# Fewer unread products ahead of the first read one, the others placed anew

## The chip, the cores and the metric

The kernel runs on one core of one Trainium2 chip. The metric is the device time of one execution in microseconds, the median of several runs. A core has several engines that run side by side, each with its own queue in a fixed order: PE multiplies matrices (its weight loads are shown as PEld), DVE, ACT and POOL work element by element, and SP issues most of the transfers (DMA). An instruction whose operands are not there makes its engine wait, and all behind it in that queue wait with it.

## The reference

The reference has two halves. The first is a gated linear recurrence with complex gates over 768 steps, for 4 batches of 8 heads with 48 channels; the second is a mixer over the tokens and a two-layer network over the 384 channels.

```python
scale = np.minimum(mag, 0.999) / (mag + 1e-06)        # mag = |a_re + i a_im|
a_re_n, a_im_n = (a_re * scale, a_im * scale)
for t in range(S):
    new_re = ar * S_re - ai * S_im                     # ar, ai: the gates of step t
    new_im = ar * S_im + ai * S_re
    S_re, S_im = (new_re + kv, new_im)                 # kv: outer product of k and v
    y[:, :, t] = np.einsum('bhd,bhde->bhe', q[:, :, t], S_re)
...
h = xt @ U @ V                                         # x: y with the heads side by side
u = x + h.transpose(0, 2, 1)
ch = np.maximum(u @ w_ch1, 0.0) @ w_ch2
return (u + ch).astype(np.float32)
```

## The kernel before

The sequence is cut into chunks of 128 steps, six to a batch, 24 in all, and two neighbouring chunks make a group. For each group `gates` turns the inputs `a_re` and `a_im` into logarithms of magnitudes and angles. `magnitudes_of` has ACT and DVE work in turn until the logarithms stand in `GL`. `within` then has PE sum them along the chunk, with the fixed matrices `mid` and `fore` as weights (L674, tiles `es ps` and `ef ps`), and ACT takes exponentials of the sums into `es` and `ef`. `of_blocks` does the same for sums over blocks (L712, `tot`, weights `total`). `angles` sums the angles along the chunk (L776 and L779, `ph`), and ACT and DVE reduce them (`F`, L782) for the sines and cosines `cs`. In the first group the two chunks go through these steps one by one.

`prep` scales queries and keys with `es` and `cs` (DVE, L377, `QKC`), PE transposes them (L834, `tr`) and ACT copies the transposes out (L845, `QK`). `chain` does the attention of the chunk: products within blocks (L881 and L884, `inner`; L948, `corners`), the state (L973, `dk`), and the chunk's output (L1004 and L1012, `y`), which ACT copies to `xo`. When the six chunks of a batch are done, `mixer` works on pairs of them: the low-rank mixing (`rank`, `mixed`, `uTp`), and the two layers (L1094 `up` or L1152 `few`; L1241 and L1284 `down`).

The weights of the two layers are loaded in pieces into a staging ring of two tiles (`stage`), and `single` has DVE and ACT put each piece into its place by five word operations (L556 to L562 in the early pieces).

What each engine does in which order is not left to a scheduler. Every operation is added to a `Plan` with its engine and kind, and the table `ORDER` gives each a place, a number; `order` sorts all operations by that place. The lists of all engines follow from the sorted list, and instructions of one engine keep that order.

The table `SPARE` belongs to the same places. An entry `37: 79` says that 79 units of unread product stand ahead of the operation at place 37. A unit multiplies 128 columns of the identity matrix by the identity; `idle` makes products of up to four units (512 columns) out of a run of units, at L1414. They read `ident` alone, write one tile in PSUM that no instruction reads, and stand in PE's queue like every other product. In float32 each product shows as two passes in the trace, each with its own weight load. Place 37 is the first read product of the program, the `es ps` sum of the first chunk.

```python
        out += [-1] * SPARE.get(at[n], 0) + [n]
...
    def idle(k):
        ...
        nc.tensor.matmul(out=spare[0][:, :k], lhsT=ident, rhs=ident.unsqueeze(1).to_broadcast([128, k, 128]), start=True, stop=True)
...
        while run:
            idle(min(run, 4))
            run -= min(run, 4)
        plan.ops[n][4]()
```

Places that the prediction names: 37, 43, 45, 46 and 56 (first group's sums: `es ps`, `ef ps` and `tot`), 84 and 93 (its angles), 113 to 122 and 144 (transposes of the first two chunks), 127 and 147 (`inner` of the first chunk), 245 and 255 (the two halves of `dk` of the second chunk), 246 (L779 of the fourth chunk), 272 and 275 (the transposes of the third chunk), 276 (`y` of the second).

## Time and profile before

| | |
|---|---|
| Runs (us) | 646.06, 649.92, 652.8 (median 649.92) |
| The profiled execution (us) | 645.24 |
| Its span (us) | 643.5 |
| PE busy | 633.6 us, 98% |
| DVE busy | 510.2 us, 79% |
| ACT busy | 398.5 us, 62% |
| Unread products (L1414) | 81 products, 162 passes, 1.4 to 126.3 us |
| First read product (L674) | 21.40 us |
| First product of the two layers (L1094) | 128.69 us |

The span runs from the first to the last instruction of the profiled execution; its time as a run is 1.7 us more. A busy share counts an engine's instructions whether or not somebody needs them, so PE's 98% holds the unread products too. The profile shows no column for the rate of one pass: the granted clock stands at 1.00 throughout, and a slower stretch of PE is read from the distance between neighbouring passes. In the timeline neighbouring instructions of one kind are merged, and a merged line shows the shape of the first alone.

### The profile page before, as it was taken

The page shows a single profiled execution, that of the slowest core. Times are in us where ns is not written, and L with a number is a line of the kernel's source. Part 1 is how long each engine was busy: PE and PEld are TensorE (multiplying, and loading weights), DVE is VectorE, ACT ScalarE, POOL GpSimd, SP SyncE. Part 2 cuts the span into 40 slices and gives each one's busy share as a digit, 9 for nine tenths or more (in the row PEclk, how much of TensorE's full clock was granted, in tenths as well). Part 3 has the DMA queues.
Part 4 walks back from the last instruction along what each step waited for, and adds up shares of the span by engine and source line. Part 5 has one row for each costly group of instructions (what it writes and reads, how often), then busy time and mean ns, then how long its engine had stood idle before and what let it go on. Part 6 is the DMA issues. An engine that isn't in the chain of part 4 may idle for free.

```text
span 643.5 us, 23479 instructions
## 1 busy us (share of the span) xinstructions
PE 633.6 (98%) x10384; PEld 535.4 (83%) x10384; DVE 510.2 (79%) x923; ACT 398.5 (62%) x765; POOL 39.1 (6%) x79
## 2 busy tenths in 40 slices
PE   9999999999999999999999999999999999999998
PEld 3566667686789988888989988888999998999997
DVE  4599999968999989768876968788999894573653
ACT  4599999888887897766868585868532422202010
POOL 5000000000001000020010000010100000000200
DMA  8367556456125341431540430521212010000101
GB/s 206 67 163 162 117 110 148 118 151 138 35 43 119 74 82 39 85 79 30 105 88 5 92 85 13 105 67 21 50 45 46 12 32 8 1 13 1 38 7 43
DMA packets 173685, 45.74 MB, mean 71 GB/s; under 512 B 167632, under 2 KB 170384, under 8 KB 173584
## 3 DMA queue, kind: packets, MB, share of 16 engines
q1 hardware_dynamic: 171376, 39.90, 29.5%
q0 software_dynamic: 2208, 4.35, 2.0%
q8 instruction: 81, 1.33, 0.9%
q14 instruction: 20, 0.16, 0.1%
HBM read 33.59 MB, written 4.72 MB: 60 GB/s over the span
## 4 chain that ended last, share of the span: by engine, by line
PE 87%; DVE 8%; issue 2%; ACT 1%; DMA 1%; SPq 0%; POOL 0%; DVEq 0%; POOLq 0%
PE down L1284 24%; PE up L1094 18%; PE few L1152 11%; PE spare L1414 5%; PE tr L834 3%; PE y L1012 3%; PE dk L973 3%; PE inner L884 3%; PE down L1241 2%; PE inner L881 2%; PE y L1004 2%; PE tot L718 2%; DVE QKC L377 2%; PE mixed L1066 1%; DVE QK L377 1%
## 5 line engine op out<-in xcount | busy, mean ns | idle before, releaser
L1094 PE MATMUL up<-uT,w 128*128 128x256 f32 x504 | 115.9, 383 | 0.0
L377 DVE TENSOR_TENSOR QK<-QK,T 112x512 f32<-112x512 f32 (+1 forms) x144 | 102.3, 730 | 7.1 <-PE inner L881 3.3
L1094 PEld LDWEIGHTS up<-uT,w 128*128 128x128 f32 x504 | 93.8, 190 | 13.0 <-ACT h L374 0.3
L1284 PE MATMUL down<-w,h 128*128 128x192 f32 x396 | 73.3, 331 | 0.0
L374 ACT ACTIVATE gate<-gate 128x768 f32<-128x768 f32 (+1 forms) x89 | 69.8, 798 | 4.9 <-DMA gate<-in_a_im_dram 1.9
L845 ACT COPY QK<-tr 112x512 f32<-112x512 f32 x96 | 52.5, 586 | 32.2 <-PE tr L834 31.2
L1284 PEld LDWEIGHTS down<-w,h 128*128 128x128 f32 x396 | 64.4, 190 | 2.5 <-issue 1.7
L1414 PE MATMUL spare<-ident 128*128 128x512 f32 (+3 forms) x162 | 62.2, 506 | 1.8 <-POOL ident masks.py:199 1.4
L1414 PEld LDWEIGHTS spare<-ident 128*128 128x128 f32 x162 | 29.4, 196 | 27.9 <-issue 21.9
L377 DVE TENSOR_TENSOR QKC<-qk,cs 128x768 f32<-128x768 f32 x48 | 45.6, 953 | 7.9 <-PE tr L834 4.4
L380 DVE TENSOR_TENSOR xo<-down,xo 128x192 f32<-128x192 f32 (+1 forms) x79 | 30.1, 386 | 24.2 <-PE down L1284 23.8
L1160 ACT COPY h<-few 128x512 f32<-128x512 f32 x30 | 17.2, 587 | 51.4 <-PE few L1152 51.4
L1284 PE MATMUL down<-stage 128*128 128x192 f32 x198 | 38.0, 332 | 0.0
L1152 PE MATMUL few<-gate,w 128*128 128x128 f32 x280 | 35.9, 276 | 0.0
L834 PEld LDWEIGHTS tr<-ident,QKC 64*112 64x112 f32 x768 | 25.6, 130 | 10.9 <-issue 4.7
L759 POOL DMA_DIRECT2D gate<-F x15 | 12.4, 823 | 355.0 <-DVE F L782 208.5
L953 ACT COPY AT<-corners 32x128 f32<-32x128 f32 x96 | 24.2, 255 | 15.4 <-PE corners L948 13.9
L1152 PEld LDWEIGHTS few<-gate,w 128*128 128x128 f32 x280 | 33.6, 192 | 0.2
L834 PE MATMUL tr<-ident,QKC 64*112 64x64 f32 x768 | 32.4, 222 | 0.9 <-ACT QK L845 0.7
L1228 POOL DMA_DIRECT2D out_dram<-xo x32 | 19.0, 613 | 231.5 <-DVE xo L380 173.4
L374 ACT ACTIVATE es<-es ps 128x384 f32<-128x384 f32 x48 | 21.9, 491 | 17.8 <-PE es ps L674 11.3
L1284 PEld LDWEIGHTS down<-stage 128*128 128x128 f32 x198 | 31.8, 190 | 0.8 <-DVE QKC L377 0.2
(156 smaller groups left out, 1251.9 us busy)
## 6 DMA issues: line engine op xcount, KB each, us to landing
stage<-in_moe_w_ch_dram SPq DMA_DIRECT2D x12, 768.0 KB, 5.4
gate<-in_a_im_dram SPq DMA_DIRECT2D x24, 192.0 KB, 3.7
gate<-in_a_re_dram SPq DMA_DIRECT2D x24, 192.0 KB, 3.3
qk<-in_q_dram SPq DMA_DIRECT2D x24, 192.0 KB, 3.2
qk<-in_k_dram SPq DMA_DIRECT2D x24, 192.0 KB, 3.2
VP<-in_v_dram SPq DMA_DIRECT2D x24, 192.0 KB, 3.4
AT<-DG SPq DMA_DIRECT2D x96, 32.0 KB, 2.1
T<-E SPq DMA_DIRECT2D x48, 48.0 KB, 2.8
```

Of the source, the lines that this page charges most:

```text
L374: return nc.scalar.activation(out=o, in_=i, func=f, **kw)
L377: nc.vector.tensor_tensor(out=o, in0=a, in1=b, op=OP.mult)
L380: nc.vector.tensor_tensor(out=o, in0=a, in1=b, op=OP.add)
L834: nc.tensor.transpose(out=get(*ps[r])[0:DQ, h], in_=get(*qkc)[at, h].rearrange("p u d -> p (u d)")[:, 0:DQ], identity=ident[at, at], tile_ ...
L845: nc.scalar.copy(out=to, in_=a)
L884: nc.tensor.matmul(out=get(*ps0)[j * BLK:(j + 1) * BLK, h, 0:3 * HB], lhsT=k_of(h, j * BLK, BLK), rhs=q_of(h, (PL, 3), (1, HB), at=j * HB) ...
L953: ACT(0.36, RR, lambda r=r, u=u: nc.scalar.copy(out=get(*ATi).rearrange("p (a u) t -> p a u t", u=2)[r:r + BLK, :, u, BLK:2 * BLK], in_=ge ...
L973: nc.tensor.matmul(out=get(*dk[r])[x:end, h], lhsT=get(*ks)[at, h, x // DP, 0:end - x], rhs=get(*VPi)[at, h], start=True, stop=True, tile_ ...
L1094: nc.tensor.matmul(out=get(*ps)[:, e], lhsT=w1[:, f, (ff + e) * 128:(ff + e + 1) * 128], rhs=get(*uT)[:, f], start=(f == 0), stop=(f == KD ...
L1152: nc.tensor.matmul(out=get(*ps)[:, q], lhsT=w()[:, q * 128:(q + 1) * 128], rhs=v[0](), start=(n == 0 and q == 0), stop=True, skip_group_ch ...
L1284: nc.tensor.matmul(out=get(*to)[:, part], lhsT=x(j), rhs=y[:, j], start=(first and j == 0), stop=(j == KH - 1), skip_group_check=not first)
L1414: nc.tensor.matmul(out=spare[0][:, :k], lhsT=ident, rhs=ident.unsqueeze(1).to_broadcast([128, k, 128]), start=True, stop=True)
```

## The change

Only the table `SPARE` is changed. At place 37 stand 20 units where 79 stood: five products of 512 columns in place of 19 of them and one of 384. Behind place 37 there were 150 units and are now 152. Of these 110 keep their places, 40 are taken away and 42 are added. Most entries change by one to six units; the largest changes are at places 272 (0 to 14) and 275 (13 to 3). The order of all other operations on every engine is the same.

```diff
-SPARE = {37: 79, 43: 1, 45: 2, 46: 1, 56: 1, 84: 14, 93: 1, 113: 10, 116: 5, 122: 5, 127: 2, 140: 1, 144: 5, 147: 4, 173: 1, 175: 1, 205: 13, 235: 1,
-         246: 1, 255: 7, 275: 13, 287: 1, 302: 2, 305: 6, 325: 3, 340: 2, 367: 3, 376: 4, 391: 2, 416: 9, 423: 1, 433: 2, 449: 2, 455: 1, 469: 2, 488:
-         11, 492: 2, 501: 1, 510: 2, 531: 1, 571: 2, 573: 2}
+SPARE = {37: 20, 43: 2, 45: 4, 56: 1, 84: 15, 93: 3, 113: 11, 116: 2, 122: 4, 127: 3, 144: 7, 147: 3, 161: 1, 170: 2, 205: 13, 245: 2, 255: 1, 272:
+         14, 275: 3, 276: 1, 302: 1, 305: 6, 325: 3, 334: 1, 340: 1, 367: 3, 376: 4, 402: 3, 416: 5, 423: 5, 433: 2, 449: 3, 469: 3, 488: 9, 492: 3,
+         501: 1, 510: 2, 534: 1, 571: 2, 573: 2}
```

## The prediction

> **What bounds the kernel now.** I read the page's busy times and slices first. PE, the matmul engine, looks like the bound over the whole span, but part of its work here is products that nobody reads, so its share says little. The slices (16.1 us each) show that DVE and ACT are half idle in the first two and then nearly full.

> ```profile
> PE 633.6 (98%) x10384; PEld 535.4 (83%) x10384; DVE 510.2 (79%) x923; ACT 398.5 (62%) x765; POOL 39.1 (6%) x79
> ...
> PE   9999999999999999999999999999999999999998
> ...
> DVE  4599999968999989768876968788999894573653
> ACT  4599999888887897766868585868532422202010
> ```

> Second, the waits between 21.4 and 45 us (engine and line, what it waited for, us in total, times, longest). The two longest are one event: ACT waits 11.3 us for the first read product (es ps, L674), and DVE waits as long for an ACT step queued behind that one.

> ```profile
> ACT es L374 <- PE es ps L674: 11.3, 1, 11.3
> DVE GL L380 <- ACT gate L374: 11.3, 1, 11.3
> ```

> Third, the timeline of the first 31 us (start, duration, both us, engine, line). PE runs 40 unread passes from 1.43 to 21.4 us. The product behind them needs GL, which DVE had finished at 9.18 + 0.56 = 9.74 us. Up to 6.71 us the weight loads (PEld) stand 0.855 us apart, from 7.46 us on 0.43 us: each pass took twice as long in the first 6 us.

> ```profile
> 1.43 20.14 PE L1414 MATMUL spare<-ident 128*128 128x512 f32 x40 [1.43 <-POOL ident masks.py:199]
> ...
> 5.86 0.34 PEld L1414 LDWEIGHTS spare<-ident 128*128 128x128 f32 x1 [0.52 <-issue]
> ...
> 6.71 0.34 PEld L1414 LDWEIGHTS spare<-ident 128*128 128x128 f32 x1 [0.52 <-issue]
> ...
> 7.46 0.19 PEld L1414 LDWEIGHTS spare<-ident 128*128 128x128 f32 x1 [0.41 <-issue]
> ...
> 7.88 0.19 PEld L1414 LDWEIGHTS spare<-ident 128*128 128x128 f32 x1 [0.24 <-issue]
> ...
> 9.18 0.56 DVE L380 TENSOR_TENSOR GL<-GL,gate 128x384 f32<-128x384 f32 x1
> ...
> 10.06 0.92 ACT L374 ACTIVATE gate<-gate 128x384 f32<-128x384 f32 x2
> ...
> 11.36 0.56 DVE L560 TENSOR_SCALAR w<-w 128x768 uint32<-128x768 uint32 x1
> ...
> 20.76 0.19 PEld L1414 LDWEIGHTS spare<-ident 128*128 128x128 f32 x1 [0.24 <-issue]
> ...
> 21.40 0.81 PE L674 MATMUL es ps<-GL,mid 128*128 128x384 f32 x2
> ...
> 22.25 0.49 ACT L374 ACTIVATE es<-es ps 128x384 f32<-128x384 f32 x1 [11.27 <-PE es ps L674]
> ```

> Last, the busy times by stretch (after the two times: the length, then busy us of PE, PEld, DVE, ACT and POOL with counts). From 32 to 130 us DVE works 27.86 + 34.09 + 32.97 = 94.92 of 98 us: there DVE sets the pace, with ACT close behind, and unread products fill what PE would have idle. From about 130 us on the read products fill PE.

> ```profile
> 11.00:21.40 10.40, 10.40 (x26) 4.64 (x25) 0.91 (x3) 0.00 (x0) 1.19 (x4) 1.00 0.38 107
> ...
> 32.00:60.00 28.00, 27.37 (x552) 17.81 (x551) 27.86 (x50) 27.06 (x48) 0.00 (x0) 1.00 0.62 144
> 60.00:95.00 35.00, 34.04 (x823) 22.55 (x822) 34.09 (x55) 33.21 (x66) 0.00 (x0) 1.00 0.58 132
> 95.00:130.00 35.00, 33.29 (x777) 24.05 (x776) 32.97 (x57) 31.94 (x61) 0.00 (x0) 1.00 0.58 140
> ```

> **Part 1: the products ahead of the first read one.** A unit is 128 columns, four units make one product, and each product is two passes. At place 37 there were 79 units (20 products, 40 passes); there are now 20 (5 products, 10 passes). When is PE free? The 40th pass loaded its weights at 20.76, and es started at 21.40, 0.64 us later. The 10th loaded at 7.88, so PE is free at about 8.52. When can es start? GL is there at 9.74; the next es followed its GL (DVE, 23.18 + 0.56 = 23.74) at 23.89, so 0.15 us later: 9.89 us. PE thus pauses 1.4 us, and es starts 11.51 us earlier than at 21.40. "mid", the other operand, was ready at 6.24 us on POOL.

> What follows on ACT: es starts on ACT 22.25 − 21.40 = 0.85 us after es on PE, so at 10.74, but ACT is busy until 10.06 + 0.92 = 10.98. So ACT goes on at 10.98 in place of 22.25: 11.27 us, the whole of its wait. DVE's own wait ends with ACT's next step (22.64 + 0.51 = 23.15, less 11.27 is 11.88), while DVE is busy until 11.36 + 0.56 = 11.92: it goes on at 11.92 in place of 23.18, 11.26 us earlier. Neither has a wait left there. What was hidden behind those 11.27 us: on POOL "total", done at 11.97, first needed by L712, which moves from 25.82 to 14.55; and transfers. The DMA engines fell quiet at 15.2 us, and DVE's first use of the second weight piece (L556) moves from 26.69 to 15.43. That is 0.2 us behind the last byte, so it still fits. SP's queue had stood from 10.68 to 25.78 waiting to refill an input area; that wait ends with DVE's work, so SP and every later load move up with it. **Term: −11.27 us.**

> **Part 2: the units behind it.** There were 150, there are 152. At 0.43 us a pass a unit costs 0.215 us, so 0.43 us more PE time in all, in a stretch where DVE sets the pace. I went through the places with the trace. In the first group the added units at 43, 45 and 93 end when the product behind them gets its operand anyway: es of the second chunk waits for GL until 23.89, L779 for F until 32.65. The added one at 113 makes the transposes up to 0.2 us late (they started at 35.73, just when QKC was there, at 34.72 + 0.96 = 35.68). The large move is at 255, 272 and 275 (7, 0, 13 become 1, 14, 3). In old times: dk (L973) comes about 1.1 us earlier; the 14 units end near 66.75, so the next transposes (L834) start there and not at 65.00; ACT reads them (L845) at 67.89, behind a table load that ends at 67.6, and they are done at 67.4. The transposes after them waited for that ACT copy at 68.6 and 69.0, before as after. So the 3 us of products shift inside time that ACT's queue covers; uncovered, the 1.75 us would be late at DVE's QK steps. The other places change by one to four units (0.2 to 0.9 us), in pairs that cancel within a few products.

> Bounds: at worst every added unit lies on the path and no removed one gives anything back. There are 42 of them, 42 × 0.215 = +9.0 us. At best PE never again holds DVE up and all DVE idleness from 32 to 130 us goes: 98 − 94.92 = 3.1, so −3.1 us. I take **+0.2 us**, the one delay found above, since the rows show DVE full and the moved units beside it.

> **Part 3: the pause.** Whether PE keeps its faster passes over a 1.4 us pause and products with gaps in them, no row of before shows: after 7.46 us PE never waits longer than 0.8 us until its work is done. The bounds are nothing, and one renewed slow spell as long as the first (1.43 to about 7.3, 5.9 us), which costs half its length, 2.9 us. I take nothing: the pause is short beside the 5.9 us it took to speed up. [...]

> **Sum.** −11.27 + 0.2 + 0 = −11.1 us. The profiled execution took 645.24 us (span 643.5 and 1.7 around it), so it would take 634.1. It was faster than all three runs shown (646.06, 649.92, 652.8); their median less the same sum is 649.92 − 11.1 = **638.8 us**.

> **Rivals.**
> A. *PE falls back to slow passes once* at the pause. For: the first passes were slow without a busy stretch behind them, and PE, with 9.83 us busy in 21.4 to 32 us, has small gaps just there. Against: the pause is a quarter of the 5.9 us. Price up to 2.9 us: 641.7.
> B. *Loads become the wait.* In the first 32 us 2.20 + 1.11 + 1.08 = 4.39 MB moved; they now have 20.7 us. At the 200 GB/s of the first 11 us that takes 22.0 us, 1.3 us too long: 640.1. Against: 7 to 11 us ran at 279 GB/s, and part of those bytes are needed only later.
> C. *The moved units land on the path.* All of the +9.0: 647.8. For: the unread products stand in PE's one queue, as at the start, and the 14 at place 272 are a long block. Against: the walk above, and the 40 units taken away elsewhere.
> D. *Slower: PE stays at slow passes* from the pause on until the dense products (L1094, 128.69 us). Working without a break at half rate, half of every microsecond is lost, so it decides from 22 us of slow passes on (22 / 2 = 11). Held to the dense products it adds the PE time from 21.4 to 130 once more, 9.83 + 27.37 + 34.04 + 33.29 = 104.5: 743. Against: PE with a backlog works without a pause, and 5.9 us of that sped it up.
> That PE's order is unchanged is excluded: in the changed kernel five products stand ahead of L674, and the other engines' orders are the same.

> **How the numbers follow.** Forecast 0.85, A 0.05, B 0.05, C 0.03, D 0.02. The range: the lower end is the profiled execution less the sum, 634.1, rounded down to 634; it holds the best bound, 649.92 − 11.27 − 3.1 = 635.6. The upper end is the slowest run shown less the sum, 641.7, with some 1.8 for part of A or C: 643.5. C in full and D are left out. A measurement of this kernel can tell about 1% (6.5 us) from no change. The forecast and A and B lie beyond that (1.7, 1.3 and 1.5%), together 0.95, of which I take off 0.08 because the three runs shown differ by 1%: faster 0.87. C and that 0.08, less a hundredth for slower: 0.10. Slower: D and that hundredth, 0.03.

> **What would show it.** Right: ten passes, then a pause of about 1.4 us; L674 at about 9.9 us; ACT's es at about 11.0 without an 11 us wait; the first L1094 near 128.69 − 11.1 = 117.6 us; everything behind it as long as before; the span near 632.4. A: weight loads again 0.85 us apart behind the pause. B: DVE L556 or ACT's input steps waiting for DMA. C: DVE or ACT waiting for PE near 54 us, where L834 now stands behind 14 units. The forecast is wrong if the first L1094 comes later than 122 us, or if the stretch behind it grows.

## Result and profile after

The median of twelve runs went from 649.45 to 641.54 us; the ratio of the kernels is 0.989, with a 95% interval of 0.9853 to 0.9928 (one disturbed run of the twelve is left out of it). In a second set of runs it was 0.9893 (0.9857 to 0.993). So the change saves about 7 us where 11.1 were forecast. The profiled execution took 638.75 us, 6.5 less than the one before, and 4.7 more than the 634.1 of the sum.

The page's slices (one digit for a fortieth of the span) show the hole of DVE and ACT in the first two slices gone:

```profile
span 637.0 us, 23399 instructions
...
DVE  6999898877999989569886868689999894573653
ACT  6899897898887887767678576777442331202010
```

The timeline of the first 25 us (start, duration, engine, line; in brackets the idle time ahead and what ended it):

```profile
1.42 7.54 PE L1414 MATMUL spare<-ident 128*128 128x512 f32 x10 [1.42 <-POOL ident masks.py:199]
...
8.53 0.94 ACT L374 ACTIVATE gate<-gate 128x384 f32<-128x384 f32 x2 [0.90 <-DMA gate<-in_a_im_dram]
...
10.29 0.56 DVE L380 TENSOR_TENSOR GL<-GL,gate 128x384 f32<-128x384 f32 x1
...
10.99 0.88 PE L674 MATMUL es ps<-GL,mid 128*128 128x384 f32 x2 [2.03 <-DVE GL L380]
...
12.00 0.47 ACT L374 ACTIVATE es<-es ps 128x384 f32<-128x384 f32 x1
...
12.94 0.55 DVE L380 TENSOR_TENSOR GL<-GL,gate 128x384 f32<-128x384 f32 x1
```

Ten passes, a pause, and es at 10.99 us where it was 21.40. ACT and DVE go on at 12.00 and 12.94 without the 11 us wait, 10.25 and 10.24 us earlier than before. Those 10 us still stand at the transposes that moved from 71.70 to 61.42 us. At the first dense product only 5.65 are left. PE's own timeline shows where they went:

```profile
61.42 0.66 PE L834 MATMUL tr<-ident,QKC 64*112 64x64 f32 x16
...
67.43 0.44 PE L834 MATMUL tr<-ident,QKC 64*112 64x64 f32 x8 [0.72 <-issue]
...
77.45 0.34 PE L881 MATMUL inner<-QK 112*16 112x16 f32 x25 [0.68 <-issue]
...
96.05 1.02 PE L973 MATMUL dk<-VP,QKC 64*48 64x48 f32 x54 [1.13 <-issue]
...
105.94 0.87 PE L718 MATMUL tot<-total,GL 128*96 128x32 f32 x8 [1.31 <-issue]
...
123.04 2.32 PE L1094 MATMUL up<-uT,w 128*128 128x256 f32 x10
```

PE stops inside runs of products whose operands are there ("issue": nothing that the profile shows was waited for). Number all that stands in PE's queue in order of time, the passes, the weight loads and 168 semaphore and drain instructions: seven such waits (0.72, 0.18, 0.68, 0.23, 1.13, 0.44 and 1.31, 4.69 us in all) stand ahead of numbers 1985, 2241, 2497, 2753, 3265, 3521 and 3777, each 193 plus a multiple of 256. In the kernel before the same stretch has one, the last of these lines; the first is ACT's step on the second chunk's a_im, there without a wait:

```profile
7.41 0.92 ACT L374 ACTIVATE gate<-gate 128x384 f32<-128x384 f32 x2
...
71.70 0.66 PE L834 MATMUL tr<-ident,QKC 64*112 64x64 f32 x16
...
88.49 1.12 PE L1414 MATMUL spare<-ident 128*128 128x512 f32 x2 [0.41 <-issue]
```

The queue row of the changed kernel's page says what has that size:

```profile
q8 instruction: 81, 1.33, 0.9%
```

1.33 MB in 81 transfers is 16,384 bytes each. PE's queue holds 20,856 entries (2 × 10,344 passes and weight loads and the 168 others); behind the first 193 that is 80.7 times 256. The kernel below with 10,232 passes shows 80 such transfers, the one with 10,420 shows 82. So I read these counts as PE getting its instructions in blocks of 256. In the trace, from 62 to 106 us, a block's transfer starts 1.1 to 4.1 us after PE has entered the block before it, takes 0.9 to 1.5 us, and PE goes on no earlier than 1.26 us after its end. The blocks ahead of the seven waits lasted 3.5 to 6.5 us, the waits at their ends included. I call these pauses block waits and add up those over 0.1 us from number 449 on.

### The profile page after: what moved, and what is told of

It reads as the page before. It is cut to its first block, busy times and chain, and to the rows that moved or that the text cites. A ratio compares the mean times of both kernels' runs of the same rounds, so it can differ in the third digit from the quotient of the medians.

```text
span 637.0 us, 23399 instructions
## 1 busy us (share of the span) xinstructions
PE 621.6 (98%) x10344; PEld 529.0 (83%) x10344; DVE 510.1 (80%) x923; ACT 399.0 (63%) x765; POOL 37.3 (6%) x79
## 3 DMA queue, kind: packets, MB, share of 16 engines
q8 instruction: 81, 1.33, 0.9%
## 4 chain that ended last, share of the span: by engine, by line
PE 88%; ACT 4%; DVE 4%; issue 2%; DMA 1%; SPq 1%; DVEq 0%; ACTq 0%
PE down L1284 24%; PE up L1094 18%; PE few L1152 11%; PE tr L834 4%; PE dk L973 4%; PE y L1012 3%; PE spare L1414 3%; PE inner L884 3%; PE down L1241 3%; PE y L1004 2%; PE inner L881 2%; PE tot L718 2%; PE mixed L1066 1%; PE uTp L1079 1%; PE corners L948 1%
## 5 line engine op out<-in xcount | busy, mean ns | idle before, releaser
L1094 PE MATMUL up<-uT,w 128*128 128x256 f32 x504 | 115.6, 383 | 0.0
L1094 PEld LDWEIGHTS up<-uT,w 128*128 128x128 f32 x504 | 94.2, 190 | 12.4
L845 ACT COPY QK<-tr 112x512 f32<-112x512 f32 x96 | 52.5, 586 | 33.7 <-PE tr L834 32.8
L374 ACT ACTIVATE gate<-gate 128x768 f32<-128x768 f32 (+1 forms) x89 | 69.8, 798 | 5.2 <-DMA gate<-in_a_im_dram 2.5
L1414 PE MATMUL spare<-ident 128*128 128x512 f32 (+3 forms) x122 | 49.4, 517 | 1.4 <-POOL ident masks.py:199 1.4
L380 DVE TENSOR_TENSOR xo<-down,xo 128x192 f32<-128x192 f32 (+1 forms) x79 | 30.2, 386 | 24.2 <-PE down L1284 23.7
L834 PEld LDWEIGHTS tr<-ident,QKC 64*112 64x112 f32 x768 | 25.8, 130 | 14.3 <-issue 5.8
L1414 PEld LDWEIGHTS spare<-ident 128*128 128x128 f32 x122 | 22.0, 199 | 18.7 <-issue 12.8
L834 PE MATMUL tr<-ident,QKC 64*112 64x64 f32 x768 | 32.8, 223 | 2.0 <-issue 0.7
L374 ACT ACTIVATE h<-up 128x512 f32<-128x512 f32 x42 | 24.6, 592 | 11.6 <-PE up L1094 11.6
```

The costliest lines, as they stand in the source:

```text
L374: return nc.scalar.activation(out=o, in_=i, func=f, **kw)
L380: nc.vector.tensor_tensor(out=o, in0=a, in1=b, op=OP.add)
L834: nc.tensor.transpose(out=get(*ps[r])[0:DQ, h], in_=get(*qkc)[at, h].rearrange("p u d -> p (u d)")[:, 0:DQ], identity=ident[at, at], tile_ ...
L845: nc.scalar.copy(out=to, in_=a)
L1094: nc.tensor.matmul(out=get(*ps)[:, e], lhsT=w1[:, f, (ff + e) * 128:(ff + e + 1) * 128], rhs=get(*uT)[:, f], start=(f == 0), stop=(f == KD ...
```

## Experiments

First the two parts by themselves, the units in another cut, and none behind the first product. The rival of the block theory is that the moved units cost the 4.7 us.

**Part 1 alone.**

```diff
-SPARE = {37: 79, 43: 1, 45: 2, 46: 1, ...   # kernel before
+SPARE = {37: 20, 43: 1, 45: 2, 46: 1, ...
```

> Only place 37 is changed (79 units to 20); behind it the units stand as in the kernel before. The changed kernel's first dense product (L1094) came at 123.04 us, 5.65 us earlier than before, though es had come 10.4 us earlier; 4.7 us went between about 62 and 106 us in eight waits of PE, each at a multiple of 256 of its passes and weight loads. Theory of the instruction blocks: PE gets its instructions in blocks of 256 (16,384 bytes a transfer) and waits when one is late, whatever stands in it; here es comes at about 10 to 11 us, and the first L1094 at 128.69 - 10.3 = 118.4 us plus whatever such waits this execution has, 0 to 5 us; the waits it has stand at multiples of 256 again, so at other operations, since the units are others. Time 637 to 644 us. Rival, the moved units: they alone cost the 4.7 us; then here no wait of that kind, first L1094 at 118.4 +- 0.5 us and a time 4.7 us below the changed kernel's.

Measured: median 641.79 us, ratio 0.9947 (0.9912 to 0.9983); es at 10.11 and the first L1094 at 124.96 us. Eight block waits, 6.00 us in all, 5.02 of them ahead of L1094; the longest, 2.0 us, stands inside "corners" (L948) and not at "tot", at the same number 3777. The moved units are not there and the loss is: the rival falls.

**Part 2 alone.**

```diff
-SPARE = {37: 20, 43: 2, 45: 4, 56: 1, ...   # changed kernel
+SPARE = {37: 79, 43: 2, 45: 4, 56: 1, ...
```

> Place 37 keeps its 79 units; behind it the units stand as in the changed kernel. Theory of the instruction blocks: es at 21.4 us as before, the first L1094 at 128.7 us plus its own block waits (0 to 5 us), the time that of the kernel before within 1%. Rival, the moved units: they cost 4.7 us here too, with waits or late products at the same operations as in the changed kernel, first L1094 at 133.4 us, time 4.7 us above before.

Measured: 649.06 us, ratio 1.0048 (1.0017 to 1.0078), first L1094 at 133.07 us, just where the rival put it. But what came late was not a product behind a unit. PE's longest waits from 22 to 135 us:

```profile
PE dk L973 <- issue: 2.6, 1, 2.6
PE inner L881 <- issue: 1.3, 1, 1.3
```

They stand at the numbers 1985 and 3521, with a third at 3265: 4.34 us. Less these, L1094 comes at 128.7 us as in the kernel before, although es had come 1.47 us earlier here (19.93 us). Most of that lead went into slow passes: the granted clock is 0.50 from 76.06 to 79.47 us, right behind the longest wait. The moved units thus cost time by way of the blocks: five products fewer stand ahead of number 1985, and the boundaries fall elsewhere.

**Products of two units.**

```diff
-            idle(min(run, 4))
-            run -= min(run, 4)
+            idle(min(run, 2))
+            run -= min(run, 2)
```

> The changed kernel with the same units at the same places, issued as products of at most two units (256 columns) in place of four: the same columns and PE time, but about 25 products, so 100 passes and weight loads, more by 67 us. Theory of the instruction blocks: every block boundary falls some 20 to 130 instructions earlier in the program; PE's waits that end by no operand stand again exactly 256 passes and weight loads apart, at other operations than L834, L884, L881, L948, L973, L881, L718 in that order, and their sum may be anything from 0 to 8 us; time 636 to 645 us. Rival, the moved units or the operations themselves: the waits stay at the same operations with the same lengths (0.7, 0.2, 0.7, 0.2, 1.1, 0.4, 1.3 us), the time stays that of the changed kernel.

Measured: 637.18 us (four runs), ratio 0.9868 (0.9815 to 0.9921). Block waits at 2753, 3521, 4289 and 8897, in other operations than in the changed kernel, 3.97 us in all: as the block theory has it. The same profile shows the prediction's rival A. The ten first products ended sooner, PE paused 2.68 us ahead of es, and soon after its passes were slow (the granted clock is 0.50 from 11.79 to 15.21 us):

```profile
10.42 0.88 PE L674 MATMUL es ps<-GL,mid 128*128 128x384 f32 x2 [2.68 <-DVE GL L380]
...
11.57 1.26 PE L674 MATMUL ef ps<-GL,fore 128*128 128x384 f32 x2
12.62 1.91 PE L1414 MATMUL spare<-ident 128*128 128x256 f32 x4
14.33 1.24 PE L674 MATMUL es ps<-GL,mid 128*128 128x384 f32 x2
15.41 0.81 PE L674 MATMUL ef ps<-GL,fore 128*128 128x384 f32 x2
```

**No unread product behind place 37.**

```diff
-SPARE = {37: 20, 43: 2, 45: 4, ...
+SPARE = {37: 20}
```

> Twenty units at place 37 as in the changed kernel, and no unread product behind it. PE has 56 products (224 passes and weight loads) less and idles where they stood. If PE keeps its faster passes (weight loads 0.43 us apart for 512 columns and the dense L1094 rows as long as before): DVE sets the pace up to 120 us, the first L1094 comes at 117 to 119 us plus block waits, time 635 to 642 us. If it falls back to slow passes wherever it idles (the rival A and D of the prediction, and the reason for such products): read products of the stretch 10 to 120 us take up to twice as long (L674 0.88 us becomes about 1.6), DVE and ACT wait for PE, and the first L1094 comes later than in the changed kernel, by up to half of PE's 70 us of read products: time 645 to 680 us.

Measured: 647.47 us, ratio 1.0038 (1.0007 to 1.0069), first L1094 at 131.47 us. The busy times by stretch (the last but two column is the granted clock) show PE idling, and its clock falling with it:

```profile
20.00:40.00 20.00, 13.59 (x265) 8.95 (x264) 18.60 (x33) 17.05 (x28) 0.00 (x0) 0.67 0.54 140
...
60.00:80.00 20.00, 15.50 (x376) 11.89 (x376) 18.04 (x32) 17.07 (x30) 0.00 (x0) 0.66 0.41 90
```

The changed kernel shows 1.00 there. So the 152 units behind place 37 are worth more than the whole gain of the change; the 59 that it takes away were the idle ones.

Next, whether the block waits come again, and what makes a block late.

**The changed kernel and the kernel before once more.**

> The changed kernel once more, with the kernel before on the same chip. So far an execution's time less its block waits (waits of PE at the multiples of 256 passes and weight loads, up to the first dense products) was 645.24 - 0.41 = 644.8 us before and 638.75 - 4.69 = 634.1 us after. Theory of the instruction blocks: the sum of the waits differs from one execution to the next, so this profile shows es at 10 to 11 us, the first L1094 at 118.3 us plus its sum, a time of 634 us plus its sum, and a sum between 1 and 8 us; the median against before lies between -4 and -11 us. Rival, the execution profiled was an odd one: its waits do not come again, the first L1094 is at 118 to 119 us.

> The kernel before once more, for its block waits. Theory of the instruction blocks: its runs lie between 643 and 653 us because the sum of its block waits differs; this execution's time less its sum is 644.8 +- 1 us, whatever its time. Rival: the kernel before has no such waits beyond the 0.4 us of its first profile, and its scatter comes from elsewhere; then a time of 649 us would show with a sum below 1 us.

Measured: 638.65 us median. The profiled execution of the changed kernel (640.21 us) has its waits ahead of the same seven numbers, 1.04, 0.46, 0.95, 0.50, 0.31, 0.64 and 1.86, in all 5.76 us. The kernel before (644.5 us) has one of 0.20. Less their waits the two took 634.45 and 644.30 us, as the first profiles did (634.06 and 644.63). So the sum is not an accident of one execution but belongs to the program; the second theory, that the scatter of the kernel before comes from such waits, was not put to the test, because this execution was one of its short ones.

**Lighter weight pieces, and no placing of the diagonal blocks.**

```diff
-                out=get("raw", p)[:, at:end].rearrange(...), in_=a.bitcast(U32)),
+                out=get("raw", p)[:, at:end].rearrange(...)[:, :, 0:n], in_=a.bitcast(U32)[:, :, 0:n]),   # n: an eighth for p > 4
```

> The changed kernel, with each weight piece from the sixth on loaded to one eighth (the other columns keep what an earlier piece left in the staging ring); every instruction of PE, DVE and ACT stays. If a block is late because data transfers stand ahead of it: with some 3 MB less between 45 and 115 us the time from entering a block to the start of the next block's transfer (median about 1.4 us, up to 4.1 in that stretch) falls below 1 us in most blocks, the block waits up to the first L1094 sum to less than 1.5 us, and the first L1094 comes at 118 to 120 us. If a block is late whatever the data do: the sum stays at 3 to 5 us and the first L1094 near 123 us.

```diff
-            SP(0.2, ("place", i), lambda js=js, to=to: nc.sync.dma_start(out=get(*ATi)[js, :, to], ...
+            continue
```

> The changed kernel without the transfers that place the diagonal blocks (AT from DG, L935, four to a chunk); those parts of AT keep zeros. The two longest delays of a block, 4.1 us each, overlapped such transfers (69.4 to 72.5 and 100.4 to 102.4 us). If those small transfers hold the blocks up: no delay over 3 us, the block waits sum to less than 2.5 us, first L1094 at 118 to 120.5 us. If not: delays of 4 us remain, the sum stays at 3 to 5 us. In both cases the y products (L1004) no longer wait for a transfer, which was 1.2 us at 257 us.

Measured: with light pieces the waits at 1985, 2241 and 2497 are gone and the one at 2753 is 0.14; those at 3265, 3521 and 3777 stay at 1.13, 0.99 and 1.86, so the sum is 4.12 up to L1094, which comes at 122.96 us. Sum and time are those of the second expectation, but four of the seven waits went all the same: the delay of the block for 2497 fell from 4.13 to 0.92 us. Without the placing transfers the two delays of 4 us remain (4.02 and 4.05) and the sum is 4.05: they are not the cause. Each of the two kernels was run once and leaves data out. So data transfers held up some blocks in these runs; what holds up the one for 3777 by 4.1 us in five profiles stays open.

**The alignment.** Fifteen small products behind the five put the boundaries back where they were before: with the units of before exactly, with the moved ones to within 20 instructions.

```diff
+        while small and plan.ops[n][0] == "PE":     # small = 15
+            nc.tensor.matmul(out=spare[0][0:64, 0, 0:32], lhsT=ident[:, 0:64], rhs=ident[:, 0:32], start=True, stop=True)
+            small -= 1
```

> The units of the kernel before, with 20 units at place 37 (five products of 512 columns), and behind those five 15 small products (64 weight columns, 32 moving columns), so that the first read product has as many passes and weight loads ahead of it as in the kernel before: every block of 256 begins at the same instruction as there, and everything comes some 10 us earlier. Theory of the alignment (which block is late in time depends on where the boundaries fall among the dense short products): block waits up to the first L1094 sum to 0 to 1 us as in the two profiles of before (0.41 and 0.00), against 5.0 us for the same units without the 15 products; first L1094 at 117.5 to 119.5 us, time 634 to 637 us. Rival, the early start itself (with 10 us less, loads and blocks meet in time): the waits stay at 3 to 6 us, first L1094 at 121 to 125 us, time 638 to 643 us.

> The changed kernel with the same 15 small products behind its five at place 37: its units and its pace, every block boundary 60 instructions earlier in the program (16 off those of the kernel before). Theory of the alignment: the seven waits move to other operations and their sum is not that of the changed kernel (4.7 and 5.8 us in two profiles); near the boundaries of the kernel before, though with its moved units, I expect 1 to 4.5 us (4.3 where the same boundaries met the moved units and the old start); time 635 to 639 us. Rival, the early start or the moved units alone: the sum stays at 4.5 to 6 us, the time at 638 to 641 us.

Measured: with the units of before 637.7 us, ratio 0.987 (0.9837 to 0.9902), three block waits of 1.40 us up to L1094, which comes at 119.56 us. PE's longest waits:

```profile
PE inner L881 <- issue: 0.7, 1, 0.7
...
PE spare L1414 <- issue: 0.6, 1, 0.6
```

Against part 1 alone (0.9912 to 0.9983) nothing differs but fifteen products of no use, and the intervals do not meet: they are worth 4 us. They also fill PE's pause ahead of es, but es comes no earlier for it (10.85 us). In the profiles the gain is block waits, 5.02 against 1.40 us, and 3.41 us at half clock that only part 1 alone has. With the moved units it is 638.27 us, 0.9892 (0.9864 to 0.9919): a single wait of 2.54 us at 1985 in place of seven, as expected. Yet the time is that of the changed kernel (0.989 and 0.9893): here the clock is 0.50 from 66.14 to 72.97 us, around that wait. The first of these is the shortest of the whole kernels with six runs or more, but its interval overlaps that of the changed kernel, so no version is shown to beat both.

**No product ahead of the first read one.**

```diff
-SPARE = {37: 20, 43: 2, ...
+SPARE = {43: 2, ...
```

> The changed kernel without any unread product ahead of the first read one. Its five products there take PE's slow start before GL is ready; without them the slow passes meet the read products from 10 us on: es takes about 1.6 us instead of 0.88, and for some 6 us PE's work takes twice as long. If PE's slow start is what the 20 units are for: ACT and DVE wait for PE there, and the twelfth to thirtieth us slip by 1 to 3 us: the first transposes (L834, 25.6 us in the changed kernel) come at 27 to 29 us. If they are idle weight, L834 starts at 25.6 +- 0.5 us as in the changed kernel. Block waits come on top in both cases, at other operations, since 20 instructions are gone.

Measured: es at 10.07 us in slow passes (1.62 us in place of 0.88), the first transposes at 27.05 us. From es to there it took 16.98 us, in the changed kernel 25.61 − 10.99 = 14.62: the slow start costs 2.4 us. The whole time, 647.25 us in a single run, says more than that, because of what comes next.

**The pause at 257 us.** In this profile and in that with the light pieces PE ran slow passes from about 260 us on, after a pause of 1.5 and 1.4 us at L1004, which waits for a placing transfer. The first line is from the light pieces' timeline, the second from its stretches; in the changed kernel the same pause (1.34 us) left the clock at 1.00.

```profile
257.61 0.67 PE L1004 MATMUL y<-VP,AT 64*64 64x48 f32 x28 [1.38 <-DMA AT<-DG]
...
260.00:265.00 5.00, 5.00 (x50) 4.78 (x49) 2.25 (x4) 2.81 (x8) 0.00 (x0) 0.50 0.01 3
```

The kernel is the one without placing transfers, shown above, now timed:

> The changed kernel without the transfers that place the diagonal blocks (those parts of AT keep zeros), timed. In two profiles PE's pause at L1004 near 257 us (1.3 to 1.4 us, waiting for such a transfer) was followed by 10 to 14 us of slow passes, 5 to 7 us of time, and in the others the same pause was not. Theory of the slow spell: without that pause there is none, and this kernel's runs lie within about 2 us of each other, where the changed kernel's lay over 5 us (637.3 to 642.6 and 636.7 to 645.2). Rival, the scatter has another source: the runs lie over 4 us or more here too.

Measured: seven runs from 634.74 to 642.28 us, six of them within 3.2 us of each other. The seventh is the one profiled. It has no pause at L1004; its slow passes follow the block wait at number 3777:

```profile
104.89 0.52 PE L718 MATMUL tot<-total,GL 128*96 128x32 f32 x4 [1.32 <-issue]
...
110.27 1.11 PE L1004 MATMUL y<-VP,AT 64*64 64x48 f32 x32
```

L1004 took 0.79 us at this place in the changed kernel. The slow passes last from about 105 to 122 us, and this execution is 6.4 us longer than the other one profiled of this kernel (635.88 us), with block waits as long. So the pause at L1004 is not the only one that can do it, and the theory was too narrow. The clock record in the traces says more. In these traces every stretch at half clock inside a program lasted a whole number of steps of 3.41 us, and those of one execution lay on one grid. Here are three steps of the second profile of the changed kernel, around its block wait of 1.86 us that ends at 106.31 us (after the two times: the length, PE's busy time; the last but two is the clock):

```profile
104.72:108.13 3.41, 1.82 (x19) 1.80 (x19) 3.37 (x7) 0.54 (x2) 0.00 (x0) 1.00 0.49 91
108.13:111.54 3.41, 3.41 (x76) 2.76 (x75) 0.00 (x0) 2.76 (x8) 0.00 (x0) 0.50 0.00 0
111.54:114.95 3.41, 3.41 (x135) 3.14 (x130) 3.31 (x6) 2.23 (x7) 0.00 (x0) 1.00 0.10 16
```

Nine profiles have 18 such falls, half of them in the kernel without units behind place 37. In the step ahead of each PE was busy for 12 to 67% of the time; of 2,339 steps at full clock that no fall followed, 15 were as idle. No slow passes followed the pause of 1.34 us at L1004 in the changed kernel, and they followed those of 1.38 and 1.50 us in the two other profiles. That it goes by what else is idle in the same step is my reading of these shares, and no experiment tested it.

The mean granted clock of each run is on record too, and 0.997 is what one step at half clock makes of 640 us. Of 57 runs of the kernel before (a 58th, of 1552.71 us, is left out) the 39 at 1.000 take 643.27 to 647.04 us, the eleven at 0.997 or less 647.24 to 650.34, and of the seven between two take 648. So its longer runs go with slow stretches, but one step costs at most 1.7 us: a part of the distance stays open.

## Why the prediction was right and wrong

The time lay in the range (641.54 us, between 634 and 643.5), the sign was right, and the gain came from where the sum had it. By its own test the prediction fails in size: the first L1094 came at 123.04 us, later than the 122 that it had named.

| kernel | start of es | time of the profile | block waits | less these | es to the first L1094 | of that at half clock |
|---|---|---|---|---|---|---|
| before | 21.40 | 645.24 | 0.61 | 644.63 | 107.29 | not on record |
| before, again | 20.89 | 644.50 | 0.20 | 644.30 | 106.79 | 0 |
| part 2 alone | 19.93 | 648.81 | 4.52 | 644.29 | 113.14 | 3.41 |
| part 1 alone | 10.11 | 641.73 | 6.00 | 635.73 | 114.85 | 3.41 |
| changed | 10.99 | 638.75 | 4.69 | 634.06 | 112.04 | 0 |
| changed, again | 9.97 | 640.21 | 5.76 | 634.45 | 114.65 | 3.41 |
| by two units | 10.42 | 637.65 | 3.97 | 633.68 | 111.95 | 3.41 |
| part 1, aligned | 10.85 | 635.75 | 1.60 | 634.15 | 108.71 | 0 |
| both, aligned | 9.79 | 638.32 | 2.69 | 635.63 | 112.93 | 6.83 |

The table holds the kernels that do the whole work with unread products at both places. The column "less these" is the prediction's world: its means are 644.4 for the first three and 634.6 for the six others, 9.8 us apart. The last two columns close the account. Take from the way between es and L1094 the block waits that stand on it and half of the time at half clock: eight of the nine then need 106.8 to 107.4 us. The ninth, part 1 alone, needs 108.1; PE waits 1.53 us for a step of DVE there, at 60.76 us. Behind L1094 all nine take 513.5 to 515.1 us.

- *Part 1, −11.27 us.* The wait was 11.27 us and all of it went, but ACT and DVE moved by 10.25 and 10.24. The step that failed here is "what was hidden behind those 11.27 us": I named POOL and two transfers and not the load of the second chunk's a_im. In this execution ACT waited 0.90 us for it (the 8.53 us line), and GL came at 10.29 where it had come at 9.18. Before, PE's queue of unread products covered any such delay; now it reaches es, which comes between 9.79 and 10.99 us. In the second profile it came at 9.97, where the sum has 9.89: there the step held.
- *Part 2, +0.2 us.* From es to the transposes at 61.42 us the lead went from 10.41 to 10.28 us: 0.13, and ACT's copies covered the 14 units as the walk had it. The table gives, less the block waits, nothing for part 2 alone, −1.3 and −1.7 for the changed kernel against part 1 alone, +1.5 for the two aligned ones: no cost of its own is shown.
- *Part 3, the pause.* 2.03 us and no slow passes behind it in the profile of the changed kernel. Rival A did not come there. By two units it did, and cost at most 1.7 us, half of a step; with nothing ahead the slow start cost 2.4. "Nothing" was too little all the same: of the 18 runs of the changed kernel 15 have a mean clock of 0.997 or less and take 637.79 to 647.58 us, the three others 636.69 to 638.75. Half clock came at idle steps later on, with block waits in them, and not at the pause that I had priced.
- *What no term held: block waits.* 4.7 and 5.8 us in place of the 0.6 and 0.2 of the kernel before. In the first profile this is most of the gap of 4.7 us to the 634.1. The page of before held the row of instruction transfers, and its timeline showed one such wait (0.41 us "issue" at 88.49 us); I took it for nothing. Removing fifteen products (two passes and two weight loads each) moved every boundary behind them by 60 instructions, and I asked only what the removed ones cost.
- *The base.* 649.92 was the median of three runs; eleven to 25 runs later in four sets had 644.82 to 646.11. The forecast of 638.8 lies 2.7 us from the first median and meets the 638.65 of the second set. That it meets the second is luck: against that set's 646.11 the base was 3.8 us too high, and the gain 3.6 too large.
- *The other rivals.* B came as the 1 us of a_im and in some blocks; C did not; D did not, though the kernel without units behind shows the clock that it feared (0.66 to 0.81 in the stretches from 20 to 131.5 us).

## What to carry to other kernels

Unread products kept PE at speed here: without those behind the first read one its clock was 0.66 to 0.81 from 20 to 131.5 us. Ahead of that product they were worth their place only up to the moment at which its operand was ready (9.74 us in the kernel before); behind that they were a queue, and ACT, which waited for the first result, showed it as one wait of 11.27 us. PE's program came in blocks of 256 instructions by the count above (81 transfers of 16,384 bytes), and an edit that adds or removes PE instructions moves every boundary behind it: fifteen products fewer moved them by 60 instructions, and the changed kernel had 4.7 and 5.8 us of waits at such places. So look for waits at equal distances in PE's instruction count before explaining a few microseconds by the edit's own place. A wait of 2.58 us at one of them (part 2 alone) was followed by 3.41 us at a clock of 0.50, so compare the granted clocks of the runs as well as their times. A cover that is taken away also covered things that were never on the path, here the load of a_im, for which ACT then waited 0.90 us; list the first loads among them.
